# Sliding-window attention with a hard-swish layer: the last quarter of w_in asked for later, batch 1's v cast block by block, its scores and values set closer together, and the sixth of hard swish moved to the output copies

## The chip, the cores and the metric

The kernel runs on one core of a Trainium2 chip. The metric is the device time of one execution in microseconds (us). The kernel before took 319.96 us in the median of three runs (319.62 to 320.59); one further execution was profiled.

A core has five instruction queues that run side by side: PE (TensorE: matmuls, and the weight loads before them, PEld in the profile), DVE (VectorE), ACT (ScalarE), POOL (GpSimd) and SP, which here only issues DMAs. Each queue runs in its own order. Engines wait for one another through semaphores. Matmuls write to PSUM, which DVE and ACT read; POOL sees SBUF alone. DMAs that POOL issues go to a software queue (q0 of the profile), those of SP to a hardware queue (q1); both are worked off by the same 16 DMA engines.

## The reference, cut to what matters

```python
# q, k, v: [8 batches, 8 heads, 576 tokens, 64], float32
scores = (q @ k.T) / 8                              # per batch and head
rel    = pos[:, None] - pos[None, :]
slope  = 2.0 ** -(h + 1)                            # of head h
mask   = (rel >= 0) & (rel < 128)
scores = where(mask, scores - slope * abs(rel), -1e9)
attn   = softmax(scores)
x      = (attn @ v)  ->  [4608 tokens, 512]         # heads side by side
h      = x @ w_in                                   # [512, 2048]
g      = h * clip(h + 3, 0, 6) / 6
out    = g @ w_out                                  # [2048, 512], float32
```

## The kernel before, in words

**Attention.** The work goes by pairs of heads: 4 pairs in each of 8 batches, so pair 0 to pair 31 (`g` in the code; `NP` is 4, and pairs 4 to 7 are batch 1). Tokens stand in blocks of 128: four full ones and a block of 64. Because of the window, a block of queries meets its own block of keys (the *diagonal* scores) and the block before (the *off* scores). `scores_diag` and `scores_off` (L335, L363) write them to one of two PSUM tiles, `score0` and `score1`, taken in turn. ACT takes the exponential into `pd` (diagonal, L425) and `po` (off; for batch 1 in one instruction of 1024 columns, L409). POOL then zeroes the upper triangle of `pd` with two affine selects (L427). `attend` (L478) multiplies by v on PE (18 matmuls of 65 columns, L455 and L463, in the order of the query blocks 0 to 4; block j needs v blocks j-1 and j), DVE divides by the sums (a reciprocal, L484, and a product, L485), and `back` (L506) turns the result on PE (L517), after which ACT or DVE copies it into `xT`.

**v.** The five blocks of batch 1's v are loaded by SP in the order 0 to 4 (L117, 256 KB each, 128 KB for the last) and cast to bf16 by POOL: blocks 0 and 1 in one cast of 1024 columns, blocks 2 and 3 in another (L206), block 4 in a third (L209). All three are issued by one call, `cast_tokens(1, "v")`, L746.

**The feed-forward layer.** Tokens are taken in 9 tiles of 512 (`nt`). A tile has 16 *up units* (`moe_up`, L548: four matmuls of 512 columns, L532; ACT `relu`, L556; DVE minimum and product, L557, into `gbuf`) and 16 *down units* (`moe_down`, L574: four matmuls, L587). Four down units make a sub-tile of 128 rows, which DVE (ACT in places) copies out of PSUM (L596, L593). The four sub-tiles of tile 0 share one PSUM bank, tag `o`, so the first down unit of a sub-tile waits for the copy of the sub-tile before. In the order of units one up unit stands between the last down unit of sub-tile 1 and the first of sub-tile 2 (`ORDER`, L599).

**The order of the work** is written out by hand. `second_batch` (L729) holds batch 1; `fill(n)` (L609) puts the next n units in; `up_begin` (L536) issues the matmuls of an up unit ahead, and the `fill` that reaches this unit adds only ACT's and DVE's part. From pair 8 on, `segment` (L794) goes on pair by pair with a fixed number of units at each place. `UP_BANKS` (L546) says which up units of tile 0 use a PSUM bank other than tag `h`.

**w_in** is loaded in four quarters of 512 columns. The first is loaded as float32 and cast; the others are POOL's DMAs, which cast on the way (L176): quarters 1, 2 and 3 (the calls at L702, L722 and L724). Up units 12 to 15 read the last quarter. **w_out** follows on the same queue in four parts (L190).

The functions that the change touches:

Of the kernel before, what the change touches and what calls it, by code (L numbers as in the profile page):

```python
# [13 lines left out]
ALU = mybir.AluOpType  # L14
ACT = mybir.ActivationFunctionType
# [3 lines left out]
def kernel(  # L19
# [9 lines left out]
    nc = tc.nc  # L29
# [378 lines left out]
    def exp_off_full(g):  # L408
        nc.scalar.activation(out=st[g, "po"].rearrange("p e j c -> p e (j c)"),  # L409
                             in_=st[g, "sco"], func=ACT.Exp, scale=scale)  # L410
# [132 lines left out]
        up_mms(nt, ms, k0, n, hps)  # L543
        begun[nt, ms] = hps, n

    UP_BANKS = {6: "o", 8: "av", 11: "o", 12: "av", 15: "o"}  # L546

    def moe_up(nt, ms):  # L548
        gts[nt] = gbuf[nt % 2]
        hps, n = begun.pop((nt, ms), (None, 0))  # L550
        if hps is None:
            tag = UP_BANKS.get(ms, "h") if nt == 0 else "h"
            hps = BANKS[tag].tile([128, NT], FP32, tag=tag, name="hps")
        up_mms(nt, ms, n, n_ks, hps)
        r6 = rpool.tile([128, NT], FP32, tag="r6", name="r6")
        nc.scalar.activation(out=r6, in_=hps, func=ACT.Relu, bias=bias3[:, 0:1], scale=1.0 / 6.0)  # L556
        nc.vector.scalar_tensor_tensor(out=gts[nt][:, ms, :], in0=r6, scalar=1.0, in1=hps,  # L557
                                       op0=ALU.min, op1=ALU.mult)

    def last_rows(nt, sub, cut=384):  # L560
        rows = ds(nt * NT + sub * 128, 128)
        osb = opool.tile([128, d_model], FP32, tag="osb", name="osb")
        for lo, hi, tag, copy, eng in ((0, cut, "o", nc.scalar.copy, nc.scalar),
                                       (cut, d_model, "h", nc.vector.tensor_copy, nc.sync)):
            ps = BANKS[tag].tile([128, hi - lo], FP32, tag=tag, name="ops",
                                 padded_shape=[128, d_model])
            for ms in range(n_ms):
                nc.tensor.matmul(ps, lhsT=gts[nt][:, ms, ts(sub, 128)],  # L568
                                 rhs=w_out_sb[:, ms, lo:hi],
                                 start=(ms == 0), stop=(ms == n_ms - 1))  # L570
            copy(out=osb[:, lo:hi], in_=ps)
            eng.dma_start(out=out[rows, lo:hi], in_=osb[:, lo:hi])

    def moe_down(nt, step):  # L574
        sub, part = divmod(step, 4)
        if nt == n_nt - 1 and sub == 3:
            if part == 3:
                last_rows(nt, sub)
            return
        if part == 0:  # L580
            if nt == n_nt - 1 and sub in (1, 2) or nt == 1 and sub == 0:
                ops[nt, sub] = ps_h.tile([128, d_model], FP32, tag="h", name="ops")
            else:
                ops[nt, sub] = ps_o.tile([128, d_model], FP32, tag="o", name="ops")
        for i in range(4):
            ms = part * 4 + i
            nc.tensor.matmul(ops[nt, sub], lhsT=gts[nt][:, ms, ts(sub, 128)],  # L587
                             rhs=w_out_sb[:, ms, :], start=(ms == 0), stop=(ms == n_ms - 1))
        if part == 3:
            rows = ds(nt * NT + sub * 128, 128)  # L590
            osb = opool.tile([128, d_model], FP32, tag="osb", name="osb")
            if nt == n_nt - 1 and sub % 2 == 0:
                nc.scalar.copy(out=osb, in_=ops[nt, sub])  # L593
                nc.scalar.dma_start(out=out[rows, :], in_=osb)
            else:
                nc.vector.tensor_copy(out=osb, in_=ops[nt, sub])  # L596
# [52 lines left out]
    def first_batch():  # L649
# [71 lines left out]
        prepare_double(1, 1, (P,), "k")  # L721
        load_w_in(2)  # L722
        prepare_double(1, 1, (P,), "q")
        load_w_in(3)  # L724
        for dp in range(2):
            for nm in "kq":
                load_double(2, dp, nm, nc.sync)

    def second_batch():  # L729
        scores_diag(NP + 0)  # L730
        exp_diag(NP + 0, 0)
        exp_diag(NP + 0, 1)
        up_begin(0, 2, n_ks, "av")
        scores_off(NP + 0)
        exp_off_full(NP + 0)
        wide_double(1, 1, "k", V)
        fill(2)
        scores_diag(NP + 1)
        exp_diag(NP + 1, 0)
        exp_diag(NP + 1, 1)  # L740
        double(1, 1, "q", 0, "o", V)
        scores_off(NP + 1)
        exp_off_full(NP + 1)
        double(1, 1, "q", 1, "av", V)
        fill(5)
        cast_tokens(1, "v")  # L746
        scores_diag(NP + 2)
        exp_diag(NP + 2, 0)
        exp_diag(NP + 2, 1)
        fill(1)  # L750
        scores_off(NP + 2)
        exp_off_full(NP + 2)
        fill(2)
        load_w_out(0)
        load_w_out(1)
        g = 2 * NP - 1
        scores(g)
        exp_diag(g, 0)
        exp_diag(g, 1)
        exp_off_full(g)  # L760
        up_begin(0, 12, n_ks, "av")
        attend(NP)
# [11 lines left out]
        attend(NP + 1)  # L774
        back(NP, "o")
        attend(NP + 2)
        up_begin(0, 14, n_ks)
        back(NP + 1, "av")
        attend(NP + 3)
        fill(2)  # L780
        back(NP + 2, "o")
        wide_double(2, 0, "k", A)
        back(2 * NP - 1, "av")
        wide_double(2, 0, "q", V)
        fill(1)
        done[0] = 2 * NP
        fill(2)
        scores(2 * NP)
# [98 lines left out]
```

## Time and profile before

| | |
|---|---|
| median of three runs | 319.96 us (319.62 to 320.59) |
| the profiled execution, its own time | 319.64 us |
| its span, first to last instruction | 317.9 us (1.7 us lie around it) |
| PE, DVE, ACT, POOL busy | 307.0, 176.1, 196.8, 138.9 us |
| granted TensorE clock | 1.000 over the span |
| PE starts up unit 4 (the tiles named below are in this order on PE) | 29.96 us |
| PE starts `attend` of pair 4 | 40.36 us |
| POOL casts v: blocks 0 and 1, blocks 2 and 3, block 4 | 30.75, 38.39, 39.50 us |
| POOL issues quarter 3 of w_in | 26.34 us, landed 36.82 us |
| v blocks 0 to 4 of batch 1 landed | 26.22, 29.17, 35.81, 38.27, 39.44 us |

How to read it: times are counted from the first instruction. The page's first part says how long each engine was busy; matmuls overlap in it, since a matmul's own duration (0.38 us for 512 columns) is longer than the step from one start to the next (0.216 us), so an engine that is 97% busy still has gaps. The page's fourth part follows the work that ended last back to its beginning. The timeline lists the instructions of one engine in order; the brackets at the end of a row give the idle time before it and what ended it. A DMA has landed when the last of the 16 engines has reported its share.

### The profile page before, as it was taken

To read this page: it belongs to the slowest core of one execution; us is meant where nothing else is said; L and a number is where in the kernel's file an instruction comes from. 1 tells how busy PE (TensorE), PEld (TensorE's weight loads), DVE (VectorE), ACT (ScalarE), POOL (GpSimd) and SP (SyncE) were. 2 spreads that over 40 slices of the span, in tenths; PEclk is the share of its full clock that TensorE was granted. 3 is DMA by queue.
4 is the path that set the end of the run, shared out by engine and by line. 5 is a ranking of instruction groups with operands and counts; after the bars stand their busy time and mean duration, and the time that the engine had idled before them with its cause. 6 is when DMAs were issued, how large, how long until landed. Compare 5 with 4: busy or idle time off the path is not lost.

```text
span 317.9 us, 6980 instructions
## 1 busy us (share of the span) xinstructions
PE 307.0 (97%) x2671; PEld 163.4 (51%) x2710; DVE 176.1 (55%) x344; ACT 196.8 (62%) x338; POOL 138.9 (44%) x247
## 2 busy tenths in 40 slices
PE   8889999999999999999999999999999999999996
PEld 3565474455554445555676644454444444444443
DVE  6677676554456654566465546564656455455510
ACT  3869986877767666766667756675764244244401
POOL 7358192674594684548463854472231000000000
PEclk9999999999999999999999999999999999999999
DMA  7999999999999999999999999934112100000112
GB/s 271 264 373 215 255 236 200 236 235 198 216 265 180 222 215 212 213 196 253 186 178 219 190 206 198 228 95 57 49 29 75 66 34 33 35 33 33 66 57 77
DMA packets 131425, 52.43 MB, mean 165 GB/s; under 512 B 118976, under 2 KB 122816, under 8 KB 131392
## 3 DMA queue, kind: packets, MB, share of 16 engines
q1 hardware_dynamic: 125648, 46.15, 69.0%
q0 software_dynamic: 3696, 3.67, 7.1%
q10 hardware_dynamic: 2048, 2.16, 2.2%
q8 instruction: 21, 0.34, 0.5%
q14 instruction: 12, 0.10, 0.1%
HBM read 36.70 MB, written 9.44 MB: 145 GB/s over the span
## 4 chain that ended last, share of the span: by engine, by line
PE 90%; ACT 3%; DVE 3%; issue 2%; POOL 0%; DVEq 0%; POOLq 0%; ACTq 0%
PE hps L532 38%; PE ops L587 37%; PE score L399 3%; PE av L463 2%; PE av L455 2%; DVE avs L485 1%; PE ops L568 1%; PE w L163 1%; ACT w_out_sb L422 1%; PE score L346 1%; PE tp L269 1%; ACT r L556 1%; DVE gbuf L557 1%; PE score L301 1%; PE score L357 1%
## 5 line engine op out<-in xcount | busy, mean ns | idle before, releaser
L556 ACT ACTIVATE r<-hps,bias 128x512 f32<-128x512 f32 x144 | 98.9, 689 | 84.2 <-PE hps L532 83.9
L557 DVE SCALAR_TENSOR_TENSOR gbuf<-r,hps 128x512 bf16<-128x512 f32 x144 | 98.8, 688 | 91.6 <-ACT r L556 90.1
L532 PE MATMUL hps<-xT,w_in_sb 128*128 128x512 bf16 (+1 forms) x623 | 142.0, 358 | 1.7 <-ACT xT L519 0.3
L587 PE MATMUL ops<-w_out_sb,gbuf 128*128 128x512 bf16 x538 | 133.8, 379 | 2.3 <-issue 1.8
L532 PEld LDWEIGHTS <-w_in_sb 128*128 128x128 bf16 x640 | 59.2, 98 | 54.0 <-issue 1.5
L587 PEld LDWEIGHTS <-gbuf 128*128 128x128 bf16 x560 | 52.4, 98 | 57.5
L427 POOL TENSOR_SCALAR_AFFINE_SELECT pd<-pd 128x512 bf16<-128x512 bf16 x48 | 29.4, 631 | 35.2 <-ACT pd L425 35.2
L436 POOL TENSOR_SCALAR_AFFINE_SELECT po<-po 128x512 bf16<-128x512 bf16 x48 | 30.1, 633 | 30.8 <-ACT po L434 30.1
L596 DVE COPY osb<-ops 128x512 f32<-128x512 f32 x33 | 22.7, 688 | 23.8 <-PE ops L587 23.7
L425 ACT ACTIVATE pd<-score,bias_d 128x512 bf16<-128x512 f32 x48 | 31.1, 683 | 6.4 <-PE score L399 6.4
L434 ACT ACTIVATE po<-score,bias_o 128x512 bf16<-128x512 f32 x48 | 33.1, 690 | 0.0
L213 POOL CAST tbuf<-ldbuf 128x512 bf16<-128x512 f32 (+1 forms) x45 | 25.7, 611 | 15.7 <-issue 14.6
L474 DVE TENSOR_TENSOR avs<-av,rc 128x384 bf16<-128x384 f32 (+1 forms) x48 | 23.6, 491 | 1.6
L463 PEld LDWEIGHTS <-pd 128*128 128x128 bf16 x192 | 14.3, 97 | 8.2 <-issue 0.2
L455 PE MATMUL av<-vbuf,po 128*128 128x65 bf16 x192 | 18.0, 193 | 0.0
L206 POOL CAST vbuf<-ldbuf 128x1024 bf16<-128x1024 f32 x14 | 14.3, 1041 | 7.6 <-DMA ldbuf<-in_v_dram 7.6
L463 PE MATMUL av<-vbuf,pd 128*128 128x65 bf16 x192 | 17.3, 194 | 0.0
L455 PEld LDWEIGHTS <-po 128*128 128x128 bf16 x192 | 14.3, 98 | 3.0 <-DVE avs L474 0.5
L439 ACT ACTIVATE p4buf<-score,bias_d 128x64 bf16<-128x64 f32 x48 | 15.6, 324 | 0.0
L399 PEld LDWEIGHTS <-kTb 64*64 64x64 bf16 x480 | 9.4, 106 | 9.1 <-issue 8.5
L399 PE MATMUL score<-qTb,kTb 64*64 64x192 bf16 (+1 forms) x480 | 13.1, 234 | 0.0
L246 POOL CAST pr<-ldbuf 128x576 bf16<-128x576 f32 x18 | 11.5, 668 | 2.6 <-PE tp L238 1.3
(107 smaller groups left out, 201.7 us busy)
## 6 DMA issues: line engine op xcount, KB each, us to landing
out_dram<-osb SPq DMA_DIRECT2D x33, 256.0 KB, 3.5
ldbuf<-in_v_dram SPq DMA_DIRECT2D x31, 256.0 KB, 4.6
ldbuf<-in_q_dram SPq DMA_DIRECT2D x20, 256.0 KB, 5.0
ldbuf<-in_k_dram SPq DMA_DIRECT2D x16, 256.0 KB, 5.3
ldbuf<-in_q_dram SPq DMA_DIRECT2D x12, 288.0 KB, 6.6
ldbuf<-in_k_dram SPq DMA_DIRECT2D x12, 288.0 KB, 6.7
w_out_sb<-in_moe_w_out_dram POOLq DMA_DIRECT2D x4, 512.0 KB, 9.1
w_in_sb<-in_moe_w_in_dram POOLq DMA_DIRECT2D x3, 512.0 KB, 8.8
```

The lines of the kernel that those rows point to most:

```text
L213: nc.gpsimd.tensor_copy(out=tbuf[:m, :, j, :], in_=s[:m, j, :, :].rearrange("p (i e) d -> p i (e d)", e=2))
L399: nc.tensor.matmul(wide[e][c, ds(at, n)], lhsT=kT[r, j, c], rhs=qT[r, ds(q0, n)], start=True, stop=True)
L425: nc.scalar.activation(out=pd[:, e, :, :], in_=block_scores(g, e, False), func=ACT.Exp, bias=bias_d[:, h:h + 1], scale=scale)
L427: nc.gpsimd.affine_select(out=pd[:, e, :, :], in_=pd[:, e, :, :], pattern=[[0, 4], [1, 128]], channel_multiplier=-1, base=0, compare_op=AL ...
L434: nc.scalar.activation(out=po[:, e, :, :], in_=sc, func=ACT.Exp, bias=bias_o[:, h:h + 1], scale=scale)
L436: nc.gpsimd.affine_select(out=po[:, e, :, :], in_=po[:, e, :, :], pattern=[[0, 4], [-1, 128]], channel_multiplier=1, base=-1, compare_op=A ...
L455: nc.tensor.matmul(out_av, lhsT=po[:, e, (qt if full(g) else qt - 1) % 4, :], rhs=vb[:, qt - 1, h, :], start=True, stop=False)
L463: nc.tensor.matmul(out_av, lhsT=d, rhs=vb[:, qt, h, :], start=(qt == 0), stop=True)
L532: nc.tensor.matmul(hps[:, lo:hi], lhsT=w_in_sb[:, ks, ts(ms, 128)], rhs=xT[:, ks, ds(src, hi - lo)], start=(ks == 0), stop=(ks == n_ks - 1))
L556: nc.scalar.activation(out=r6, in_=hps, func=ACT.Relu, bias=bias3[:, 0:1], scale=1.0 / 6.0)
L557: nc.vector.scalar_tensor_tensor(out=gts[nt][:, ms, :], in0=r6, scalar=1.0, in1=hps, op0=ALU.min, op1=ALU.mult)
L587: nc.tensor.matmul(ops[nt, sub], lhsT=gts[nt][:, ms, ts(sub, 128)], rhs=w_out_sb[:, ms, :], start=(ms == 0), stop=(ms == n_ms - 1))
```

## The change

- `load_w_in(3)` moves from the end of `first_batch` to a place in `second_batch` behind the affine selects of pair 5.
- `cast_tokens(1, "v")` is replaced by five calls of `cast_v`, one cast of 512 columns (L200) for each block: blocks 0 and 1 ahead of pair 5's affine selects, block 2 ahead of pair 6's, blocks 3 and 4 behind these and ahead of pair 7's.
- The scores of pairs 6 and 7 and `attend` of pair 4 come earlier among the units: ahead of `attend(4)` PE has up units 4 to 7 where it had 4 to 12. Units are put between the later steps instead. At the end of `second_batch` two units fewer have been issued, and every unit from there on stands two places later in `segment`.
- `back` of pair 6 follows that of pair 5 directly.
- Hard swish is computed without its sixth: ACT gives `relu(h + 3)`, DVE the minimum with 6 and the product; the copies out of PSUM multiply by 1/6 (ACT with an activation instead of a copy, DVE with a tensor-scalar operation instead of a copy). For up units 5 and 6 of tile 0, DVE does both steps: one tensor-scalar operation in place of ACT's.
- Units 6, 12 and 15 of tile 0 are given the banks `o`, `o` and `av`.

```diff
-        nc.vector.memset(bias3, 0.5)
+        nc.vector.memset(bias3, 3.0)
...
-    UP_BANKS = {6: "o", 8: "av", 11: "o", 12: "av", 15: "o"}
+    UP_BANKS = {6: "o", 12: "o", 15: "av"}
...
-        nc.scalar.activation(out=r6, in_=hps, func=ACT.Relu, bias=bias3[:, 0:1], scale=1.0 / 6.0)
-        nc.vector.scalar_tensor_tensor(out=gts[nt][:, ms, :], in0=r6, scalar=1.0, in1=hps,
+        if nt == 0 and ms in (5, 6):
+            nc.vector.tensor_scalar(out=r6, in0=hps, scalar1=-3.0, scalar2=3.0,
+                                    op0=ALU.max, op1=ALU.min)
+            nc.vector.scalar_tensor_tensor(out=gts[nt][:, ms, :], in0=r6, scalar=3.0, in1=hps,
+                                           op0=ALU.add, op1=ALU.mult)
+            return
+        nc.scalar.activation(out=r6, in_=hps, func=ACT.Relu, bias=bias3[:, 0:1], scale=1.0)
+        nc.vector.scalar_tensor_tensor(out=gts[nt][:, ms, :], in0=r6, scalar=6.0, in1=hps,
                                        op0=ALU.min, op1=ALU.mult)
+    def sixth_scalar(out, in_):
+        nc.scalar.activation(out=out, in_=in_, func=ACT.Copy, scale=1.0 / 6.0)
+    def sixth_vector(out, in_):
+        nc.vector.tensor_scalar(out=out, in0=in_, scalar1=1.0 / 6.0, scalar2=0.0,
+                                op0=ALU.mult, op1=ALU.add)
...
# first_batch
         prepare_double(1, 1, (P,), "q")
-        load_w_in(3)
# second_batch, from the fill behind pair 4's scores; g is 4
         fill(2)
+        cast_v(1, 0, P)
+        cast_v(1, 1, P)
         scores_diag(g + 1); exp_diag(g + 1, 0); exp_diag(g + 1, 1)
+        load_w_in(3)
         double(1, 1, "q", 0, "o", V)
         scores_off(g + 1); exp_off_full(g + 1)
         double(1, 1, "q", 1, "av", V)
-        fill(5)
-        cast_tokens(1, "v")
+        cast_v(1, 2, P)
+        fill(2)
         scores_diag(g + 2); exp_diag(g + 2, 0); exp_diag(g + 2, 1)
-        fill(1)
+        cast_v(1, 3, P)
+        cast_v(1, 4, P)
         scores_off(g + 2); exp_off_full(g + 2)
-        fill(2)
+        fill(1)
+        scores_diag(g + 3); exp_diag(g + 3, 0); exp_diag(g + 3, 1)
         load_w_out(0)
         load_w_out(1)
-        scores(g + 3); exp_diag(g + 3, 0); exp_diag(g + 3, 1); exp_off_full(g + 3)
-        up_begin(0, 12, n_ks, "av")
+        scores_off(g + 3); exp_off_full(g + 3)
+        up_begin(0, 7, n_ks, "av")
         attend(g)
         fill(1)
+        up_begin(0, 8, n_ks)
+        attend(g + 1)
+        fill(1)
         prepare_double(2, 0, (A, P))
...
-        up_begin(0, 13, n_ks)
-        attend(g + 1)
-        back(g, "o")
         attend(g + 2)
-        up_begin(0, 14, n_ks)
-        back(g + 1, "av")
+        back(g, "o")
+        fill(1)
         attend(g + 3)
-        fill(2)
+        back(g + 1, "av")
         back(g + 2, "o")
+        fill(1)
         wide_double(2, 0, "k", A)
+        fill(1)
         back(g + 3, "av")
         wide_double(2, 0, "q", V)
-        fill(1)
+        fill(2)
         done[0] = 2 * NP
         fill(2)
```

(In the diff, lines that belong to one step are joined by semicolons, and `g + 1` stands for `NP + 1` on both sides.)

More of the change, by code (lines that the diff above doesn't have):

```diff
@@ L562, in last_rows @@
         osb = opool.tile([128, d_model], FP32, tag="osb", name="osb")
-        for lo, hi, tag, copy, eng in ((0, cut, "o", nc.scalar.copy, nc.scalar),
-                                       (cut, d_model, "h", nc.vector.tensor_copy, nc.sync)):
+        for lo, hi, tag, copy, eng in ((0, cut, "o", sixth_scalar, nc.scalar),
+                                       (cut, d_model, "h", sixth_vector, nc.sync)):
             ps = BANKS[tag].tile([128, hi - lo], FP32, tag=tag, name="ops",
@@ L592, in moe_down @@
             if nt == n_nt - 1 and sub % 2 == 0:
-                nc.scalar.copy(out=osb, in_=ops[nt, sub])
+                sixth_scalar(osb, ops[nt, sub])
                 nc.scalar.dma_start(out=out[rows, :], in_=osb)
             else:
-                nc.vector.tensor_copy(out=osb, in_=ops[nt, sub])
+                sixth_vector(osb, ops[nt, sub])
                 nc.sync.dma_start(out=out[rows, :], in_=osb)
@@ L729, in second_batch @@
     def second_batch():
-        scores_diag(NP + 0)
-        exp_diag(NP + 0, 0)
-        exp_diag(NP + 0, 1)
+        g = NP
+        scores_diag(g)
+        exp_diag(g, 0)
+        exp_diag(g, 1)
         up_begin(0, 2, n_ks, "av")
-        scores_off(NP + 0)
-        exp_off_full(NP + 0)
+        scores_off(g)
+        exp_off_full(g)
         wide_double(1, 1, "k", V)
         fill(2)
-        scores_diag(NP + 1)
-        exp_diag(NP + 1, 0)
-        exp_diag(NP + 1, 1)
+        cast_v(1, 0, P)
+        cast_v(1, 1, P)
+        scores_diag(g + 1)
+        exp_diag(g + 1, 0)
+        exp_diag(g + 1, 1)
+        load_w_in(3)
         double(1, 1, "q", 0, "o", V)
-        scores_off(NP + 1)
-        exp_off_full(NP + 1)
+        scores_off(g + 1)
+        exp_off_full(g + 1)
         double(1, 1, "q", 1, "av", V)
-        fill(5)
-        cast_tokens(1, "v")
-        scores_diag(NP + 2)
-        exp_diag(NP + 2, 0)
-        exp_diag(NP + 2, 1)
+        cast_v(1, 2, P)
+        fill(2)
+        scores_diag(g + 2)
+        exp_diag(g + 2, 0)
+        exp_diag(g + 2, 1)
+        cast_v(1, 3, P)
+        cast_v(1, 4, P)
+        scores_off(g + 2)
+        exp_off_full(g + 2)
         fill(1)
-        scores_off(NP + 2)
-        exp_off_full(NP + 2)
-        fill(2)
+        scores_diag(g + 3)
+        exp_diag(g + 3, 0)
+        exp_diag(g + 3, 1)
         load_w_out(0)
         load_w_out(1)
[L756 to L760, printed above, removed]
-        up_begin(0, 12, n_ks, "av")
-        attend(NP)
+        scores_off(g + 3)
+        exp_off_full(g + 3)
+        up_begin(0, 7, n_ks, "av")
+        attend(g)
+        fill(1)
+        up_begin(0, 8, n_ks)
+        attend(g + 1)
         fill(1)
@@ L772, in second_batch @@
         load_tokens(3, "q")
-        up_begin(0, 13, n_ks)
-        attend(NP + 1)
-        back(NP, "o")
-        attend(NP + 2)
-        up_begin(0, 14, n_ks)
-        back(NP + 1, "av")
-        attend(NP + 3)
-        fill(2)
[L781 to L784, printed above, removed]
-        fill(1)
+        attend(g + 2)
+        back(g, "o")
+        fill(1)
+        attend(g + 3)
+        back(g + 1, "av")
+        back(g + 2, "o")
+        fill(1)
+        wide_double(2, 0, "k", A)
+        fill(1)
+        back(g + 3, "av")
+        wide_double(2, 0, "q", V)
+        fill(2)
         done[0] = 2 * NP
```

## The prediction, on record before the run

> **What bounds the kernel now.** I read the page first: busy time by engine, then the chain that ended last.
>
> ```profile
> PE 307.0 (97%) x2671; PEld 163.4 (51%) x2710; DVE 176.1 (55%) x344; ACT 196.8 (62%) x338; POOL 138.9 (44%) x247
> ...
> PE 90%; ACT 3%; DVE 3%; issue 2%; POOL 0%; DVEq 0%; POOLq 0%; ACTq 0%
> ```
>
> PE is the bound, and its work (2710 matmuls) is the same after the change. The time can move only by PE's gaps. Taking starts of matmuls, those beyond a shape's usual step sum to some 2.7 us from 30 us on, so hardly more than that can be gained; a new wait of PE costs its full length. Next I read batch 1 on PE and POOL, in the timelines.
>
> ```profile
> 29.96 4.48 PE L532 MATMUL hps<-xT,w_in_sb 128*128 128x512 bf16 x19
> ...
> 40.36 0.23 PE L463 MATMUL score<-vbuf,gbuf 128*128 128x65 bf16 x2
> ...
> 46.19 0.45 PE L517 MATMUL tb<-ident,avs 128*128 128x128 bf16 x5 [0.34 <-DVE avs L485]
> ```
>
> ```profile
> 30.75 1.04 POOL L206 CAST vbuf<-ldbuf 128x1024 bf16<-128x1024 f32 x1
> 38.39 1.04 POOL L206 CAST vbuf<-ldbuf 128x1024 bf16<-128x1024 f32 x1 [6.60 <-DMA ldbuf<-in_v_dram]
> 39.50 0.61 POOL L209 CAST vbuf<-ldbuf 64x512 bf16<-64x512 f32 x1
> 40.06 1.21 POOL L427 TENSOR_SCALAR_AFFINE_SELECT gbuf<-gbuf 128x512 bf16<-128x512 bf16 x2
> ```
>
> PE computes up units 4 to 8 from 29.96 (20 matmuls, of which 19 were recorded) and reaches `attend(4)` at 40.36. POOL waits 6.6 us for v, then casts blocks 2 and 3 (landed at 35.81 and 38.27) and block 4 (landed at 39.44) until 40.11. So v is in place just when PE arrives: the nine up units ahead of `attend(4)` hide the load.
>
> **Part 1: `attend(4)` comes sooner than v.** After the change four up units stand there. PE's arrival: 29.96 + 16 matmuls of 0.216 us = 3.46; the scores of pairs 6 and 7 cost 0.33 + 0.87 each (34.37 to 34.70 and 35.57 to 36.44), together 2.41; two changes of matmul shape ahead of them 0.2; the off scores of pair 7 wait about 0.13 for ACT, which frees their bank. Sum 36.2. The query blocks that need only v blocks 0 and 1 are done by 36.5. The rest waits for the casts of blocks 2, 3 and 4.
>
> When do these land? In the trace the software queue's quarters 1 and 2 of w_in land at 29.83 and 33.17, quarter 3 at 36.82. While they run, an engine sends packets of w_in (1 KB) and v (256 B) one for one, 32 pairs in the 3.65 us from 33.17 to 36.82, so 0.114 us a pair; w_in's packet has 0.098 us of it, 3.1 us for the 32 of a quarter. On 14 of the 16 engines v is ahead; two lag by 2 us, and they set the landing (block 2: 32.59 at the latest on the 14, 35.45 and 35.81 on the two). At 33.17 the last one still has 23 packets of block 2, 64 of block 3 and 32 of block 4, 119 in all, by its later landings. Left alone it would send them at 26 to 36 ns each (64 between 36.82 and 38.27 with 9 gone ahead, 32 in 1.17 us), until 36.5. Quarter 3 is asked for behind pair 5's affine selects: those end at 30.8 in before; the casts of blocks 0 and 1 (0.61 each, block 1 landed at 29.17) put them 0.3 later, to 31.1. From POOL's issue to the first packet it took 3.5 us (21.05 to 24.54) and 2.1 us (41.23 to 43.33): first packets at 33.2 to 34.6. That is behind 33.17 but ahead of 35.4, when only 32 packets of v would be left; from any start before that, all of quarter 3 goes between v's packets, and block 4 lands again at about 39.4. **The later request gives block 2 up to 1.5 us and block 4 next to nothing.**
>
> The Trainium skill ("DMA: Bandwidth & Descriptors", "Latency and other measured facts") gives a software-queue DMA about 1 us to its first byte; by that quarter 3 would start at 32, and v would gain nothing at all. It also says that two of the engines (7 and 15) are usually slower; the trace has two that lag.
>
> So block 4 lands at 39.44, its cast (0.61; between 0.61 and 1.04, the rows of L209 and L206; same shape as L209's, so 0.61) ends at 40.11, PE goes on at 40.17 and has `attend(4)` done at 40.26, against 40.91. By then it has done units 4 to 7 where it had 4 to 12: 20 matmuls x 0.216 = 4.32 us less. Net 4.32 - 0.65 = **+3.67 us**. Everything later queues behind this; POOL's affine selects of pair 7 run behind the cast at 40.1 to 41.3, ahead of `attend(7)` (42.7), so they add nothing, and w_out is asked for at the old time.
>
> **Part 2: the backs.** The wait at 46.19 (0.5 us from start to start, and 0.08 at the back before) ends with a product of DVE. After the change `back(6)` stands directly behind `back(5)`; DVE has a reciprocal (0.21), a product (0.82) and one up unit (0.69) for each pair between. Following its queue with these rows gives 0.67 there against 0.56: **+0.1 us**.
>
> **Part 3: two units later from pair 8 on.** Here the lines are those of DVE and PE around 70 us.
>
> ```profile
> 69.97 1.03 PE L532 MATMUL hps<-xT,w_in_sb 128*128 128x512 bf16 x4
> 71.25 1.03 PE L587 MATMUL ops<-w_out_sb,gbuf 128*128 128x512 bf16 x4
> 72.12 1.03 PE L532 MATMUL hps<-xT,w_in_sb 128*128 128x512 bf16 x4
> ```
>
> ```profile
> 69.81 0.69 DVE L596 COPY osb<-ops 128x512 f32<-128x512 f32 x1 [0.32 <-PE ops L587]
> 72.14 0.69 DVE L557 SCALAR_TENSOR_TENSOR gbuf<-r,hps 128x512 bf16<-128x512 f32 x1 [1.63 <-ACT r L556]
> 72.74 0.19 DVE L473 RECIPROCAL rc<-av 128x6 f32<-128x6 f32 x1
> 72.96 0.56 DVE L474 TENSOR_TENSOR avs<-av,rc 128x384 bf16<-128x384 f32 x1
> ```
>
> The down unit at 68.96 closes sub-tile 1 of tile 0; DVE copies it at 69.81, idle until then, and the unit at 71.25 opens sub-tile 2 in the same bank, long free. Two places later the unit in the place of 71.25 closes sub-tile 1, and the one behind the next up unit, at 72.98, opens sub-tile 2. The copy now queues on DVE behind the rows at 72.14 (which waits for ACT, busy with exponentials and two copies), 72.74 and 72.96; it runs from 73.45 to 74.14, and PE goes on at 74.18: **+1.2 us**. Going on in the same way through the order of both kernels, the other waits of PE between 50 and 96 us sum to 2.52 us after and 2.14 before (for before this agrees with the trace's gaps to a few hundredths each); most of the difference is two waits, 0.52 and 0.32 where 0.33 and 0.13 stood: **+0.4**. Behind that the pattern repeats, and two more units at the end of the PE queue are work that was only put off.
>
> **Parts at nothing.** The sixth: the copies out of PSUM become tensor-scalar operations of the same 128x512 float32. No row shows that. By DVE's tensor-scalar rows at the start (256 columns of bf16 in SBUF, 0.22 to 0.63) twice the columns would take 0.44 to 1.26; the copy itself and DVE's product, both of 512 columns from PSUM, take 0.688. I take 0.69, the rows of the same size and source. At 1.26 the copy that PE waits for in part 3 would end 0.6 later; at 0.44, 0.25 sooner. The same bounds hold for the first step of units 5 and 6. On ACT the nearest rows are the copy, 0.585, and an activation, 0.689: 0.1 more, for three copies of the last tile. The very last one (0.48 at 314.03) ends its DMA about 0.5 us ahead of DVE's, which covers 0.1. Units 5 and 6 move 0.69 us each from ACT to DVE; DVE has that room between 31 and 36 us, as there is nothing for it but the products of these units. Six casts or three, POOL is waiting for v either way.
>
> **Sum:** 3.67 + 0.1 + 1.2 + 0.4 = 5.4 us; unrounded 5.3. On the profiled execution's own 319.64 us (span 317.9 and 1.7 around it) that is 324.9. The median shown is 0.3 above this execution, so I forecast **325.2 us** for a median.
>
> **Rivals.**
> (B) v lands early. If quarter 3's first packets come after 35.4, or its packets give way, block 4 lands at 36.5 or sooner. With v in place at PE's arrival, parts 1 and 2 shrink to 0.5, and part 3 stays: +2.1; with block 4 at 36.5, +2.6. That is 322.0 to 322.6, up to 324 for landings between. For it: this is what the order needs. Against: the two queues shared each engine one for one until 36.8. 20%.
> (C) The clock falls. PE would be all but idle from 36.5 to 40.17, with 4 matmuls of 0.03 us in between; the trace has no gap over 0.6 us behind its start. There, with the granted clock lower, matmuls of 512 columns take 0.427 us a step from 1.43 to 7.2 us, then 0.216. Such a stretch costs up to half its 5.8 us: 325.2 + 2.9 = 328.1. The Trainium skill ("TensorE: Matmul & The Clock Gate", "Part 1: The HAM clock gate (the "warmup" mystery)") says that one idle window of about 3.4 us halves the clock; by an estimate from that page 3.4 us at half speed lose 1.7 us. The windows run free and ours is barely longer. 7%.
> (D) Faster. Place: PE's waits for DVE between 42 and 96 us, 2.7 us in all. If v is in place by 36, and the two-place lag puts up units where those waits are, so that they vanish, the time is 319.96 - 2.7 = 317.3 at best. It decides at the copy of sub-tile 1: done before 72.98 or not. The rows above speak against both halves. 8%: half of it faster, half within 0.3%, which is about what a measurement of this kernel can tell from no change (0.96 us).
> The forecast (A), with its size open by block 4's landing (38.9 to 39.6) and by 0.3 to 0.6 us in part 3, is 324.3 to 326.1: 65%.
>
> **Numbers.** The range that holds A and most of B: 321.8 to 326.4, about 82%. Faster 0.04, same 0.04, slower 0.92.
>
> **What would show it.** In the timelines of the changed kernel: POOL's cast of block 4 starting at 39.5 behind a wait for `in_v_dram`; PE's row of L463 in `attend(4)` with over 2 us idle, released by POOL, in two pieces (about 39.0 and 40.2); a wait of over 1 us of a down unit for DVE near 76 us; a chain that ended last with 90% PE still, and a longer idle of PE in the groups of L463 and L587. I am wrong on part 1 if block 4's cast begins before 37, on part 3 if the down unit has no such wait, and on both in size if the granted clock falls after 40 us.

## The result, and the profile after

The changed kernel takes 321.64 us in the median of 20 runs (321.14 to 323.87), the kernel before 320.07 us on the same chip (20 runs, 319.59 to 322.07). The ratio is 1.0052, with a 95% interval of 1.0037 to 1.0066: slower, by 1.2 to 2.1 us, where 5.2 were forecast. The time lies 0.2 us under the range given, 0.4 us below rival B (322.0 to 322.6), the nearest of the cases, and 2.7 us below the forecast A (324.3 to 326.1). One run of the kernel with the request last (326.22 us) counts as slow and is left out of its figures below; all other runs count as fast.

The profiled execution took 321.32 us (span 319.6) against 319.64 (span 317.9): 1.7 us more, the same as the medians say. So its trace can be set against that of before. Counted from the first scores of pair 5 (L372, 29.39 us before, 29.41 after) to the last matmul's start it is 285.28 against 286.94 us: all of the 1.7 us come after that point.

The page of the changed kernel, busy time by engine and the chain that ended last:

```profile
PE 306.8 (96%) x2672; PEld 163.3 (51%) x2710; DVE 177.1 (55%) x346; ACT 195.9 (61%) x336; POOL 139.0 (44%) x249
...
PE 83%; DMA 8%; DVE 3%; issue 2%; ACT 1%; SPq 1%; POOL 1%; ACTq 0%; DVEq 0%
```

PE has the same work in more time, so the loss is in its gaps. The chain has 8% of DMA, where it had none. Followed back, it runs from a back at 41.60 through DVE's product (40.72) into a load of q (issued at 33.55), from there through POOL's mask and its cast of v's block 1 (29.58) into loads that began before 21 us. Most of this isn't idle time of PE: a chain tells which event came last, not how long anybody waited for it. What v cost is read from POOL's timeline (columns as in the prediction: start, duration, engine, line, operation, and in brackets the idle time before and what ended it):

```profile
29.58 0.62 POOL L200 CAST vbuf<-ldbuf 128x512 bf16<-128x512 f32 x1 [1.47 <-DMA ldbuf<-in_v_dram]
30.15 1.22 POOL L427 TENSOR_SCALAR_AFFINE_SELECT gbuf<-gbuf 128x512 bf16<-128x512 bf16 x2
31.31 0.76 POOL L176 DMA_DIRECT2D w_in_sb<-in_moe_w_in_dram  x1
33.91 0.61 POOL L200 CAST vbuf<-ldbuf 128x512 bf16<-128x512 f32 x1 [1.84 <-DMA ldbuf<-in_v_dram]
34.48 1.22 POOL L427 TENSOR_SCALAR_AFFINE_SELECT gbuf<-gbuf 128x512 bf16<-128x512 bf16 x2
35.65 1.16 POOL L200 CAST vbuf<-ldbuf 128x512 bf16<-128x512 f32 x2
```

Block 2 is cast at 33.91, when it has landed (33.85); blocks 3 and 4 landed at 34.76 and 35.28 and are cast together from 35.65, without waiting for any DMA. What holds them is the mask of pair 6 (34.48 to 35.70), which stands ahead of them on POOL. Before, these three blocks landed at 35.81, 38.27 and 39.44. The prediction had the cast of block 4 at 39.5, and named "before 37" as the sign that its first part is wrong.

PE at the backs of pairs 5 and 6, and around 72 us, with DVE beside it:

```profile
40.60 0.44 PE L517 MATMUL tb<-ident,avs 128*128 128x128 bf16 x5
41.60 0.45 PE L517 MATMUL tb<-ident,avs 128*128 128x128 bf16 x5 [0.56 <-DVE avs L485]
```

```profile
70.68 1.03 PE L532 MATMUL hps<-xT,w_in_sb 128*128 128x512 bf16 x4
72.66 1.02 PE L600 MATMUL ops<-w_out_sb,gbuf 128*128 128x512 bf16 x4 [0.96 <-DVE osb L570]
```

```profile
70.62 0.69 DVE L563 SCALAR_TENSOR_TENSOR gbuf<-r,hps 128x512 bf16<-128x512 f32 x1 [2.57 <-ACT r L562]
71.23 0.19 DVE L473 RECIPROCAL rc<-av 128x6 f32<-128x6 f32 x1
71.45 0.56 DVE L474 TENSOR_TENSOR avs<-av,rc 128x384 bf16<-128x384 f32 x1
71.93 0.68 DVE L570 TENSOR_SCALAR osb<-ops 128x512 f32<-128x512 f32 x1
```

The down unit that opens sub-tile 2 waits for the copy of sub-tile 1, and this copy stands on DVE behind a product, a reciprocal and another product, the very rows the prediction named (it put them near 76 us, with v late). PE's matmul starts tell what this costs: 71.33 to 72.66 is 1.34 us, 1.12 more than the usual step.

All waits of PE that changed, as the excess of a start-to-start time over the usual step of that shape (us; the time in the first column is the start of the matmul ahead of the wait):

| place after | released by | before | after |
|---|---|---|---|
| scores of pair 7, 34.15 | ACT (bank) | 0.15 | 0.31 |
| `attend(4)`, 36.63 | POOL, cast of block 4 | none | 0.21 |
| back of pair 6, 40.82 (before: of pair 7) | DVE product | 0.50 | 0.72 |
| up unit, 51.98 | DVE | 0.30 | 0.37 |
| at 56.77 and 87.28 before | DVE, PE | 0.48 | none |
| up unit, 61.67 | DVE | 0.34 | 0.19 |
| down unit, 71.33 | DVE copy | none | 1.12 |
| values, 78.22 | ACT | 0.12 | 0.33 |
| back and up unit, 90.13 and 91.03 | DVE, ACT | 0.77 | 0.96 |
| sum | | 2.66 | 4.21 |

The difference is 1.55 us, of 1.7. So the theory to test: v lands ahead of PE, and what makes the kernel slower is a few short waits, above all the copy at 72. Two things were to be shown besides: why v lands 4 us sooner, and what the change would have cost had it not.

The runs of the kernel before differ a little from chip to chip, so each kernel below is set against those of its own chip: 320.45 us beside the first four kernels (early request, two units, two up units apart, sixth alone), 320.47 beside the second four, 319.89 beside the request a microsecond sooner. By this measure the changed kernel stands at +1.6.

### The profile page after: what moved, and what is told of

It is laid out like the page before. It is cut to its first block, busy times and chain, and to the rows that moved or that the text cites. A ratio compares the mean times of both kernels' runs of the same rounds, so it can differ in the third digit from the quotient of the medians.

```text
span 319.6 us, 6985 instructions
## 1 busy us (share of the span) xinstructions
PE 306.8 (96%) x2672; PEld 163.3 (51%) x2710; DVE 177.1 (55%) x346; ACT 195.9 (61%) x336; POOL 139.0 (44%) x249
## 3 DMA queue, kind: packets, MB, share of 16 engines
q0 software_dynamic: 3696, 3.67, 7.1%
## 4 chain that ended last, share of the span: by engine, by line
PE 83%; DMA 8%; DVE 3%; issue 2%; ACT 1%; SPq 1%; POOL 1%; ACTq 0%; DVEq 0%
PE ops L600 37%; PE hps L532 36%; DMA ldbuf<-in_k_dram 4%; PE score L399 3%; DMA ldbuf<-in_v_dram 3%; PE av L463 2%; DMA ldbuf<-in_q_dram 2%; PE av L455 2%; PE ops L581 1%; DVE gbuf L563 1%; SPq L105 1%; ACT r L562 1%; PE tp L269 1%; DVE osb L570 0%; DVE qTb L287 0%
## 5 line engine op out<-in xcount | busy, mean ns | idle before, releaser
L562 ACT ACTIVATE r<-hps,bias 128x512 f32<-128x512 f32 x142 | 97.6, 689 | 86.0 <-PE hps L532 84.0
L563 DVE SCALAR_TENSOR_TENSOR gbuf<-r,hps 128x512 bf16<-128x512 f32 x142 | 97.2, 686 | 91.0 <-ACT r L562 89.9
L436 POOL TENSOR_SCALAR_AFFINE_SELECT po<-po 128x512 bf16<-128x512 bf16 x48 | 30.2, 633 | 33.5 <-ACT po L434 32.9
L570 DVE TENSOR_SCALAR osb<-ops 128x512 f32<-128x512 f32 (+1 forms) x34 | 23.0, 675 | 33.2 <-PE ops L600 26.8
L206 POOL CAST vbuf<-ldbuf 128x1024 bf16<-128x1024 f32 x12 | 12.2, 1041 | 0.4 <-DMA ldbuf<-in_v_dram 0.4
```

The costliest lines, as they stand in the source:

```text
L436: nc.gpsimd.affine_select(out=po[:, e, :, :], in_=po[:, e, :, :], pattern=[[0, 4], [-1, 128]], channel_multiplier=1, base=-1, compare_op=A ...
```

## Experiments on v's landing

**The request at its old place.** The changed kernel, with one edit:

```diff
         prepare_double(1, 1, (P,), "q")
+        load_w_in(3)
...
-        load_w_in(3)
         double(1, 1, "q", 0, "o", V)
```

> The changed kernel with one thing undone: the last quarter of w_in is asked for at its old place, ahead of batch 1. Theory: in the changed kernel v's block 4 lands at 35.3 us instead of 39.4 only because this quarter is out of the software queue; so here blocks 2 to 4 land at about 35.8, 38.3 and 39.4 again, PE waits for POOL's casts in attend(4) for 3.3 to 3.5 us, and the time is 3.0 to 3.4 us over the changed kernel: 324.6 to 325.0. Rival 1 (the forecast's step: where quarter 3 is asked for makes no difference to v): no wait there, block 4 at 35.3, time as the changed kernel, 321.6.

Measured: 326.33 us (5 runs, 325.31 to 327.24), ratio to the kernel before 1.018 (1.0156 to 1.0205), or +5.9. So the later request is worth some 4.3 us to the changed order. Its timeline shows PE waiting for v in `attend(4)` three times:

```profile
38.65 0.19 PE L463 MATMUL score<-vbuf,gbuf 128*128 128x65 bf16 x1 [1.27 <-POOL vbuf L200]
...
40.38 0.19 PE L463 MATMUL score<-vbuf,gbuf 128*128 128x65 bf16 x1 [1.45 <-POOL vbuf L200]
...
41.20 0.19 PE L463 MATMUL score<-vbuf,gbuf 128*128 128x65 bf16 x1 [0.54 <-POOL vbuf L200]
```

Blocks 2, 3 and 4 landed at 37.93, 39.51 and 40.49, and PE had come to `attend(4)` at 37.00. This is the prediction's forecast A, made by force. But it is 1.3 us slower than the theory's upper figure (0.9 when the kernel before is set at 320.45), of which more below.

**The request alone.** The kernel before, with only the request moved, behind the mask of pair 5:

```diff
-        load_w_in(3)          # at the end of first_batch
...
         exp_diag(NP + 1, 1)
+        load_w_in(3)
```

> The kernel before with one edit: the last quarter of w_in is asked for behind the mask of pair 5, at about 30.8 us instead of 26.34; order of TensorE, casts and hard swish as before. Theory (v's packets are slow only while w_in's are moving, and a quarter asked for 4.5 us later starts when v's are through): block 4 of v lands near 35.3 us, not 39.44, and GpSimd's wait of 6.6 us ahead of the cast of blocks 2 and 3 shrinks to below 3 us; the quarter lands near 38, ahead of unit 12 at 40.9; since TensorE comes to the values only at about 40, the time stays at 320.1 to 320.4. The prediction on record for this step (block 4 at 39.4 again, whatever the request) would show block 4 at 38 to 40.

Measured: 320.35 us (12 runs, 319.61 to 322.01), -0.1, ratio 0.9989 (0.9968 to 1.0010): no change, as expected, since PE isn't at v before 40. The landings are another matter, half a hit and half a miss. POOL's timeline:

```profile
31.18 0.76 POOL L176 DMA_DIRECT2D w_in_sb<-in_moe_w_in_dram  x1
31.94 1.05 POOL L206 CAST vbuf<-ldbuf 128x1024 bf16<-128x1024 f32 x1
35.30 1.04 POOL L206 CAST vbuf<-ldbuf 128x1024 bf16<-128x1024 f32 x1 [2.31 <-DMA ldbuf<-in_v_dram]
38.85 0.61 POOL L209 CAST vbuf<-ldbuf 64x512 bf16<-64x512 f32 x1 [2.50 <-DMA ldbuf<-in_v_dram]
```

Block 3 came 3 us sooner than before (35.18), block 4 only at 38.79, though the quarter was asked for at the same time as in the changed kernel. So "asked for at 31.3" does not by itself give v at 35.3. The packets say what does. Counts of packets started in half a microsecond, over the 16 engines (v: 256 B, w_in: 1 KB):

| from us | before, v | w_in | after, v | w_in | request alone, v | w_in |
|---|---|---|---|---|---|---|
| 31.0 | 76 | 67 | 103 | 65 | 59 | 76 |
| 31.5 | 73 | 78 | 319 | 29 | 67 | 75 |
| 32.0 | 79 | 75 | 446 | 14 | 176 | 55 |
| 32.5 | 79 | 78 | 342 | 8 | 334 | 32 |
| 33.0 | 78 | 74 | 201 | 8 | 314 | 23 |
| 33.5 | 74 | 76 | 94 | 56 | 211 | 42 |
| 34.0 | 116 | 69 | 49 | 90 | 175 | 52 |
| 34.5 | 307 | 37 | 3 | 101 | 92 | 77 |
| 35.0 | 186 | 25 | 0 | 99 | 74 | 76 |

At 31.5 us, of v's 4608 packets 1386 were left before and 1454 after: no difference yet. Then quarter 2 runs out on most engines. Before, quarter 3 follows at once, and v goes on at 75 packets in half a microsecond, one for one with w_in's. After, nothing follows for 2 us, and v goes at up to 446. When the quarter's packets come, at about 33.5, 2.2 us behind the issue at 31.31, 146 packets of v are left. In the execution with the request alone, all loads ran late: the first packet of v at 23.55 and not 22.63. Quarter 2 ended later, and when the quarter's packets came (about 33.4) some 900 of v's were still to go; the last 484 of them, from 34.5 on, went one for one again. The gap between the quarters is what v uses. How much of v fits in it seems to hang on the start of the loads: of the four traces with the request at 30.7 to 31.5 us, three have v's first packet at 22.63 to 22.71 and block 4 at 35.20 to 35.56, and this one has 23.55 and 38.79. No experiment moved the start of the loads by itself.

**A microsecond sooner.** The changed kernel with the request ahead of the mask of pair 5:

```diff
         cast_v(1, 1, P)
+        load_w_in(3)
         scores_diag(g + 1)
...
-        load_w_in(3)
```

> The changed kernel with the request of w_in's last quarter one step earlier on GpSimd: behind the cast of block 1, at about 30.2 us, ahead of the mask of pair 5, not behind it at 31.3. Theory (a cliff: over the ten executions profiled so far, what decides is how long behind v's first packet the quarter's first packet moves; at 9.0 to 9.6 us block 4 lands 15.2 to 17.0 us behind v's first packet, at 9.8 us and more 12.5 to 13.8 us): here the quarter's first packet moves about 9.0 us behind v's, so block 4 lands at 38 us or later, attend of pair 4 waits 2 us and more, and the time is 324.0 to 326.3, nearly that of the kernel with the quarter asked for at its old place. Rival (the landing moves with the request in proportion, 1.1 us of the 4.9 us between the two places, of a difference of 4.7 us): 322.4 to 323.0.

Measured: 323.42 us (6 runs, 321.24 to 324.44), ratio 1.0103 (1.0080 to 1.0126), or +3.5. It lies between the two forecasts, and the trace doesn't tell them apart. The profiled execution was the fastest, at 321.24, and in it the edit had no effect: POOL waited for block 1 of v, and the request came out at 31.46.

```profile
30.90 0.62 POOL L200 CAST vbuf<-ldbuf 128x512 bf16<-128x512 f32 x1 [2.95 <-DMA ldbuf<-in_v_dram]
31.46 0.77 POOL L176 DMA_DIRECT2D w_in_sb<-in_moe_w_in_dram  x1
```

Block 4 landed at 35.20 there. The other five runs took 322.78 to 324.44; where their requests went out isn't known. The longest of them shows a granted clock of 0.994 over its span, as runs with long waits for v do (below), the others 1.000. What stands is that this place costs some 2 us more than that of the changed kernel, and that the moment of the request hangs on block 1's landing. Whether there is an edge or a slope stays open. (The expectation's measure, the 1025th packet of w_in as the quarter's first, is also a poor one: two engines still send quarter 2 then. The counts above are better.)

**The request last.** The changed kernel with `load_w_in(3)` behind `cast_v(1, 4, P)`.

> The changed kernel with the last quarter of w_in asked for behind the cast of block 4, at about 36.8 us instead of 31.3. Theory: v was already through before the quarter's first packets, so block 4 lands at 35.3 again and the wait for its cast stays at 0.2 us; the quarter lands 6.8 us behind its issue, at 43.6, and unit 12, which starts at about 43 us, waits up to 0.6 us: 321.6 to 322.3. If w_in's packets still cost v something, block 4 lands before 35.0 and the time falls under 321.4.

Measured: 323.35 us (7 runs, 321.33 to 324.75), or +2.9 by the medians; the ratio of 1.0068 (1.0034 to 1.0102) says +1.1 to +3.3. Half of it is a miss. v did as the theory says: block 4 landed at 35.89, with no packet of the quarter before 37, and POOL cast blocks 3 and 4 at 35.99 without a wait. But the quarter, issued at 37.10, landed at 46.48, 9.4 us later and not 6.8, and PE waited for it: in the trace from 45.18 on, 1.29 us more than the usual step. Its first packet started only at 41.1, 4.0 us behind the issue, and from 37 us on SP's loads for batch 2 (2304 B packets) use the engines. PE also waits 0.56 us at 63.8 for a cast of the next batch's v, which the changed kernel doesn't. So the request can be too late as well: v gains nothing by it, and the quarter is late.

## Experiments on the waits

**The clock.** In the kernel with the early request the table of stretches shows more than the waits (columns: stretch, its length, busy time and instructions of PE, PEld, DVE, ACT, POOL, then the granted clock, the DMA share, GB/s):

```profile
37.19:41.26 4.07, 0.81 (x17) 0.52 (x14) 0.00 (x0) 0.78 (x2) 3.06 (x6) 1.00 1.09 308
41.26:41.65 0.39, 0.39 (x5) 0.23 (x5) 0.09 (x1) 0.00 (x0) 0.39 (x1) 1.00 1.04 384
41.65:45.06 3.41, 3.19 (x44) 2.71 (x43) 2.70 (x6) 1.82 (x3) 3.41 (x7) 0.50 1.00 308
45.06:47.00 1.94, 1.94 (x34) 1.47 (x33) 1.54 (x4) 1.33 (x2) 1.94 (x4) 1.00 1.15 191
```

Between 37.19 and the up unit at 41.29, 4.1 us, PE started 11 matmuls of 65 columns (the x17 of the row also counts those still running at its edges). Behind them the granted clock is 0.50 for 3.41 us. This is rival C. It isn't in every run: over their spans the five runs show 0.995, 0.999, 0.990, 0.994 and 0.995, and the one at 0.999 is the fastest (325.31 us). In all 20 runs of the changed kernel it is 0.999 or more. From the up unit behind `attend(4)` to the next one behind a back took 3.83 us (41.29 to 45.12), in the changed kernel 2.24 (36.95 to 39.19): 1.6 us. The Trainium skill ("TensorE: Matmul & The Clock Gate", "Part 1: The HAM clock gate (the "warmup" mystery)") says that one idle window of about 3.4 us halves the clock; the trace agrees with the length, 3.41 us, and shows that a few tiny matmuls in between don't prevent it. To test that idleness is the cause, the waits of this kernel were filled (the request stays at its old place):

```diff
+        if g == NP:
+            idle = BANKS["o"].tile([128, NT], FP32, tag="o", name="idle")
         for qt in qts:
+            if g == NP:
+                for _ in range((0, 0, 6, 7, 2)[qt]):
+                    nc.tensor.matmul(idle, lhsT=ident, rhs=w_in_sb[:, 0, 0:NT], start=True, stop=True)
```

> The changed kernel with the quarter asked for early (326.33 us), and 15 idle products of 128x512 in attend of pair 4, into a bank that holds nothing: 6 ahead of the first use of block 2, 7 ahead of block 3, 2 ahead of block 4, 3.2 us of TensorE that lie inside the 3.26 us of waits. They compute nothing that is used. Theory (of the 4.7 us between that kernel and the changed one 3.1 are waits, the rest is the clock at half for 3.4 us behind them): the granted clock stays at 1.0 behind the values, the waits end where they did, and the time falls by 1.3 to 1.7 us, to 324.6 to 325.0. Rival (the clock has nothing to do with the idle time, or the rest is something else): 326.3, or later by what of the 3.2 us does not fit the waits.

Measured: 324.91 us (6 runs, 324.39 to 325.48), ratio 1.0125 (1.0098 to 1.0152), 1.4 us faster for 15 matmuls more. The granted clock is 1.00 in every stretch from 36 to 46.5, and 0.999 or more over the span of all six runs; two of the stretches:

```profile
40.50:42.00 1.50, 1.50 (x33) 1.15 (x32) 1.42 (x3) 0.61 (x2) 1.50 (x3) 1.00 1.05 389
42.00:43.50 1.50, 1.50 (x27) 1.03 (x24) 1.47 (x4) 1.50 (x4) 1.50 (x4) 1.00 1.04 228
```

From up unit to up unit the same stretch takes 2.23 us (40.28 to 42.51). Part of the difference of the two profiled executions is that v landed sooner in this one (block 4 at 38.77, not 40.49); the stretch from unit to unit is free of that. So the early request's cost closes: counted from the first scores of pair 5 to the last matmul its execution is 4.4 us longer than the changed kernel's; 3.5 of that are PE's waits for v (three of 1.44, 1.62 and 0.70 against one of 0.21), 1.6 the clock, and 0.7 goes off, the back's wait, which is gone there.

**The two units.** The changed kernel with four units behind the second batch, where the changed kernel has two:

```diff
         second_batch()
-        fill(2)
+        fill(4)
         segment(2 * NP, G, lambda g: FILLS.get(g, (1, 1, 1, 2, 0, 1, 2)))
```

> The changed kernel with the fill between second_batch and pair 8's segment at four units instead of two, so that every unit from there on stands at the place that it has in before. Theory: what is lost behind pair 8 comes from the two places alone; the wait of 1.1 us of a down unit for DVE's copy near 71 us goes, the other waits fall back to before's, and the time is 1.3 us under the changed kernel: 320.3 (0.3 over before). Rival 2 (the waits depend on something else that the change did, such as the copies with 1/6): time as the changed kernel, 321.6.

Measured: 321.05 us (12 runs, 320.09 to 322.91), ratio 1.0024 (1.0004 to 1.0044), or +0.6: 1.0 less than the changed kernel's +1.6, where 1.3 were expected. The two intervals (+0.1 to +1.4, +1.2 to +2.1) overlap a little, so the trace has to carry the point. In the profiled execution the waits of 1.12 us and at 78 us are gone, and that at 90 us is back at 0.31. From the first scores of pair 5 (at 30.76 here, as the loads began late) to the last matmul it took 285.94 us, against 286.94 in the changed kernel: 1.0 us less again, so the lag of two units is the cause of these waits.

**Two up units between the down units.** The changed kernel with "UUDDUDD" for "UDUDUDD" in the third group of `ORDER`.

> The changed kernel with two up units instead of one between the last down unit of sub-tile 1 and the first of sub-tile 2 of tile 0 (the third group of its order UUDDUDD instead of UDUDUDD); all other units stay two places late. Theory: the wait of 1.1 us for the one PSUM bank goes to about 0.1, the rest stays: 1.1 us under the changed kernel, 320.5. Rival 2: the wait moves to the next down unit and the time stays at 321.6.

Measured: 320.74 us (12 runs, 320.31 to 322.57), ratio 1.0017 (1.0001 to 1.0034), or +0.3: 1.3 less than the changed kernel, where 1.1 were expected. The wait at the down unit is gone. The down unit at 71.71 closes sub-tile 1, DVE copies it from 73.82 to 74.50, and the down units behind the two up units start at 74.56 (second row, no bracket; the view ends at 76 us):

```profile
72.57 1.89 PE L532 MATMUL hps<-xT,w_in_sb 128*128 128x512 bf16 x8
...
74.56 1.67 PE L600 MATMUL ops<-w_out_sb,gbuf 128*128 128x512 bf16 x7
```

Its profiled execution was the longest of the twelve (322.57): block 1 of v landed at 33.24 and held up POOL, and PE waited 1.37 and 0.44 us in `attend(4)`.

**The sixth alone.** The kernel before with the new hard swish, all up units on ACT.

> The kernel before with the hard swish of the change alone (relu of h + 3, minimum with 6, the sixth in the copies out of PSUM; units 5 and 6 still by ACT). Theory: the copies cost on DVE what they did (0.69 us), on ACT 0.1 more where it is covered: time as before, 320.1, within 0.3. Rival 2 (the operations with 1/6 are longer and hold up PSUM banks): 0.6 to 1.6 us over before, 320.7 to 321.7.

Measured: 320.39 us (12 runs, 319.51 to 320.99), -0.1, ratio 0.9999 (0.9982 to 1.0016). By form, DVE's tensor-scalar takes 688 ns as the copy did, and ACT's scaled copy 597 for the plain copy's 585 (512 columns) and 491 for 479 (384):

```profile
L564 DVE TENSOR_SCALAR osb<-ops 128x512 f32<-128x512 f32 x33 | 22.7, 688 | 23.8 <-PE ops L594 23.7
L561 ACT ACTIVATE osb<-ops 128x512 f32<-128x512 f32 x2 | 1.2, 597 | 9.1 <-PE ops L594 6.3 <-remote 2.8
L561 ACT ACTIVATE osb<-ops 128x384 f32<-128x384 f32 x1 | 0.5, 491 | 2.0 <-PE ops L575 2.0
```

**All waits at once.** The changed kernel with its units laid otherwise; `up_next(0)` opens the next up unit:

```diff
-    UP_BANKS = {6: "o", 12: "o", 15: "av"}
+    UP_BANKS = {6: "o", 7: "av", 12: "o", 15: "av"}
...
-        up_begin(0, 7, n_ks, "av")
+        fill(1)
+        up_next(0)
         attend(g)
         fill(1)
-        up_begin(0, 8, n_ks)
+        up_next(0)
         attend(g + 1)
...
         back(g, "o")
-        fill(1)
+        up_next(0)
         attend(g + 3)
+        fill(1)
         back(g + 1, "av")
-        back(g + 2, "o")
         fill(1)
+        back(g + 2, "o")
         wide_double(2, 0, "k", A)
-        fill(1)
         back(g + 3, "av")
         wide_double(2, 0, "q", V)
-        fill(2)
         done[0] = 2 * NP
-        fill(2)
+        fill(4)
         scores(2 * NP)
...
         second_batch()
-        fill(2)
+        fill(4)
```

> The changed kernel with its units laid otherwise: one unit more ahead of the values of pair 4, the openings of units 8 and 9 ahead of the values of pairs 4 and 5 and of another ahead of pair 7, the backs of pairs 5 and 6 behind a unit each, and four units, not two, behind the second batch. So TensorE reaches v at about 37, not 36.2, the back of pair 5 comes 2 us behind its values, not 1, and the up units run two further ahead of the down units. Theory (the changed kernel's 1.6 us are these waits, 1.1 at the down unit, 0.7 at the back, 0.3 to 0.4 at the values and the bank, and nothing else): all of them go but the bank's, and the time is 319.6 to 320.0; where v lands a microsecond late, up to 320.8. Rival (the order of the values costs by itself, by the clock or by VectorE): 321.0 to 321.6.

Measured: 319.82 us (12 runs, 319.13 to 321.08), ratio to the kernel before 0.9972 (0.9952 to 0.9993): faster than the kernel before by 0.2 to 1.5 us (-0.7 by the medians), and so some 2.2 us faster than the changed kernel. The chain of waits is near all PE again (89%, DMA 2%), and of what the changed kernel added in the table above only the bank's 0.31 is left; the back waits 0.06, the values of pair 4 and the down unit not at all. The profiled execution was not one of the fastest (320.36): PE waited 1.1 us at 186 us for a transposing DMA of a later batch, which none of the profiled executions of before, of the changed kernel or of the kernel with the sixth alone shows. One profile doesn't tell how often that comes; six of the twelve runs are below 319.6 and six above 320.1.

## Why the prediction was wrong, step by step

**Part 1, block 4 again at about 39.4 (+3.67 us): failed**, and with it the size of the whole. Its frame was right: PE came to `attend(4)` at 36.20 (36.2 forecast), the engines share one for one while both queues run, the quarter's packets came 2.2 us behind the issue (33.2 to 34.6 forecast, about 33.5 found). The failed step is the rate of v's packets left alone, "26 to 36 ns each (64 between 36.82 and 38.27 ...)", so that the last engine's 119 packets would last to 36.5 and 35.4 be the time that decides. Those rows were not v alone: from 35 us on the trace of before has 26 to 73 packets of 2304 B in each half microsecond, of SP's next loads. In the changed kernel, between 32.0 and 32.5, a packet of v takes 18 ns (median), where beside w_in's it takes 31. At 18 ns each the prediction's 119 packets last from 33.17 to 35.3 (an estimate), and block 4 landed at 35.28; the time when only 32 are left moves from 35.4 to 34.7. The working also followed the two lagging engines alone and did not count that on the others the gap between the quarters opens at 31.5: when quarter 3's first packets came, at about 33.5 as forecast, 146 packets of v were left on all engines together, and the last of them started at 34.54. And it set landings against starts of packets, though block 4 landed 0.74 us behind the start of v's last packet in the changed kernel and 1.5 us (37.92 to 39.44) in the kernel before. One thing stays open: quarter 3's first packets still came ahead of 34.7. Whether they met the last of v's on the same engine can't be told, as the trace doesn't name a packet's engine.

The price put on a late v was about right: 3.67 us were forecast, with PE at `attend(4)` at 36.2 and block 4 at 39.44; with the early request these were 37.00 and 40.49, about a microsecond later each, and the three waits sum to 3.76 us.

So the term of 3.67 us measured 0.37: 0.21 us for block 4's cast, behind the mask and not behind the DMA, and 0.16 more at the bank.

**Quarter 3's first packets.** By the counts they moved 2.1 to 2.4 us behind the start of POOL's issue in the changed kernel, in that with the request alone and in that with a unit more ahead, 2.9 us with two up units apart and 4.0 with the request last. By the rule quoted from the Trainium skill ("DMA: Bandwidth & Descriptors", "Latency and other measured facts", about 1 us) they would have started at 32 and left v no gain; here the measurement decides.

**Part 2 (+0.1): right in place**, 0.22 found (0.72 for 0.50).

**Part 3: right where it named its wait**, +1.2 forecast and 1.12 found, at the same instruction and behind the same three rows of DVE; the two experiments that take the lag or the order away take it away. The +0.4 for the other waits didn't come: those of the table between 50 and 96 us sum to 1.85 after and 2.01 before.

**The sixth at nothing: right.** The tensor-scalar takes 688 ns; the row of the same size and source was the right one of the two bounds.

**Rival B, v early:** happened, with 1.7 us found for 2.1: 0.59 for the 0.5 of parts 1 and 2, 1.12 for the 1.2, and -0.16 for the 0.4. **Rival C, the clock:** did not happen in the changed kernel, whose longest wait for v was 0.21 us; it did in four of five runs where the wait was made by force, and cost 1.6 us in the trace, not the 2.9 given as the upper bound. The prediction gave A 65% without it and C 7%; with v late by 3.5 us, the two go together. **Rival D, faster:** its second half, a layout in which the waits vanish, exists, but it is another order than that of the change.

What stays open: how far v's landing varies in the changed kernel, whose runs go from 321.14 to 323.87. That the longest are those with late loads would fit what the other kernels' traces show, but was not shown in the changed kernel itself.

## What to carry to other kernels

Before taking a packet rate from a trace as the rate of a load "alone", look at what else the engines sent in that stretch, in both queues; the rate here was 26 to 36 ns a packet for 18, and it turned a loss of 1.6 us into one of 5. Delaying a load helps another one only by the gap that it opens, so count the packets that fit into this gap, on all engines, and look at more than one execution: the start of the loads varied by 1.7 us here. When units are taken away from a place, follow them to where they end up: here most of the loss was not at the place that the change speaks of, but 30 us on, where a lag of two units put a copy behind other work of DVE.

## What the runs showed of the hardware

- 11 matmuls of 65 columns in 4.1 us did not keep the clock up: granted 0.50 for 3.41 us behind them. With 15 idle matmuls of 512 columns in the same place it stayed at 1.00, and the kernel was 1.4 us faster (medians of five and six runs).
- With both queues running, 256 B packets of the hardware queue and 1 KB packets of the software queue went one for one, about 75 each in half a microsecond; left alone, the 256 B packets went at up to 446.
- The start of the loads varied by 1.7 us over the eleven traces (first packet of batch 1's v at 22.47 to 24.18 us). With the request at 31.2 to 31.3 us, block 4 landed at 35.28 where v's first packet came at 22.63, and at 38.79 where it came at 23.55; one trace of each.
